# A retention layer with a two-matrix ELU block: one more first-GEMM product by quarter products, with ScalarE seeding the rounds

## The chip, the core and the metric

The kernel runs on one core of a Trainium2 chip. The metric is the time of one execution on the device in microseconds (us); of several runs the median counts. The engines are TensorE (PE: matmuls, which accumulate in PSUM), VectorE (DVE) and ScalarE (ACT) (elementwise work and copies out of PSUM and into it), GpSimd (POOL) and SyncE (SP, which here issues all DMAs). Each engine works through its own instructions; they wait for one another by semaphores.

## What is computed

```python
def _attn_ref(q, k, v):                       # B, H, S, D = 4, 8, 768, 64
    gamma = 1.0 - 2.0 ** (-5.0 - np.arange(H))
    state = zeros(B, H, D, D)
    for t in range(S):
        state = gamma * state + einsum('bhd,bhe->bhde', k[:, :, t], v[:, :, t])
        y[:, :, t] = einsum('bhd,bhde->bhe', q[:, :, t], state) / sqrt(D)

def _moe_ref(x, w_in, w_out):                 # x: 3072 tokens x 512, from y
    h = x @ w_in                              # w_in: 512 x 2048
    g = np.where(h > 0, h, np.exp(np.minimum(h, 0)) - 1)
    return g @ w_out                          # w_out: 2048 x 512
```

All of it is float32. A float32 matmul of the program shows in the profile as two MATMUL records, so counts in the profile are twice those of the code.

## The kernel before

The 3072 tokens are six blocks of 512. A retention step makes each block's x in chunks of 128 tokens: scores, states and outputs, small matmuls at L319, L359, L415 and L430, which the program scatters among the GEMMs. Block 0 and block 1 go first. Blocks 2 to 5 are joined to two large blocks of 1024 tokens, and the change lies in the loop over these two (`nb`, L1659 on), with small changes in block 1 so that retention steps fit.

Both GEMMs of a large block are split by Strassen and Winograd's scheme: seven products of half size, M1 to M7, in place of eight. C11 = M1 + M2, and the others add M6, M7, M5, M4, M3 to partial sums of these. The first GEMM of a large block does three of the seven, M2, M3 and M7, *by quarter products*: each is split by the same scheme once more. `big_twice` (L1146) does one half of such a product, in this order: quarter products 1, 2, 6 and 7, then 5, then 4, then 3, each of two matmuls of 128x256, with ScalarE copies out of PSUM (`lift`, L1170) and VectorE additions (`plus`, L1174) between them. It is a generator: the loop over `ORDER1` interleaves two of them, so that products 4 and 3 of one (its tail) come among the products of the next: 1, [4], 2, 6, 7, [3], 5. Product 6 accumulates in the PSUM bank that product 1 filled, so it must wait until ScalarE has copied product 1 out.

The other four, M1, M6, M4 and M5, are done plainly, in eight rounds (L1738 on). Round n handles one eighth of the features, tile n: `rest(n, j)` (L1206) is product j, two matmuls of 128x512. M1 starts the bank `qa`, M6 accumulates on it; ScalarE copies the bank (`seed`, L1672) to a second one, `qd`, on which M4 accumulates while M5 accumulates on `qa`. `sum_` (L1215, VectorE) adds the finished M2, M3 or M7 tile on the way out. The ELU of a tile is `begin` (L1221 and L1222: a Relu and an Exp by ScalarE into one of three tiles `r`) and `end` (L1223, VectorE). T3 = C22 - C12, an input of the second GEMM, is formed by `big_t3` (L1226) between the rounds.

`second_big` is the second GEMM of a large block: seven products in the order of `ORDER2`, each by seven quarter products (L1254) of four 128x256 matmuls. `next_big_input` (L1236) makes its inputs T2, T1 and T4 in place on VectorE, `input_parts` (L891 and L1127) their quarter sums. Retention steps of the next large block are put at its `VISITS`, loads of chunks at `LOADS`.

Nothing is scheduled by a planner: every engine gets its instructions in the order in which the program emits them (`manual_schedule`). The weights' sums are made on the chip (`combine_small` for the quarter products), sent to DRAM scratch (`send_small`) and fetched again into a ring of eight slots in the order of `want_first` and `want_second` (L829), the next fetch being issued when a product is done with its slot (`done`). For the first large block the plain parts are still in SBUF (`w_all`).

Of the kernel before, what the change touches and what calls it, by code (L numbers as in the profile page):

```python
# [19 lines left out]
def kernel(  # L20
# [764 lines left out]
    ORDER2 = [1, 2, 6, 7, 5, 3, 4]  # L785

# [19 lines left out]
    def want_second(tb):  # L806

        rest = []
        for j in ORDER2:
            mine = []  # L810
            for k in (1, 2, 6, 7, 5) + ((4, 3) if j == 4 and tb == NTB - 1 else (3, 4)):
                if k in SMALL:
                    n = SMALL[k]
                    mine.append(((tb, j, k), scratch2[SEVEN[j]][:, 512 * n : 512 * n + 512]))
                else:
                    mine.append(((tb, j, k), scratch[4 * SLOT[j] + {1: 0, 2: 1, 4: 3}[k]].rearrange("p c -> p c")))
            for x in mine[:2] + rest + mine[2:5]:
                want(*x)
            rest = mine[5:]
# [3 lines left out]
    blocked = {(2, "t", 7)}  # L823
# [14 lines left out]
    W_IN = {2: w_a_[:, :, :, 1], 3: w_x_[:, :, :, 1], 7: w_x_[:, :, :, 0]}  # L838
    AMONG = {2: 0, 3: 1, 7: 2}

    def combine_small(j):

        if j == 7:
# [30 lines left out]
    LAYER = {1: w_a_[:, :, :, 0], 4: w_b_[:, :, :, 1], 5: w_b_[:, :, :, 0], 6: w_y_}  # L874
    PLANE = {1: 0, 6: 1, 5: 2, 4: 3}
# [184 lines left out]
    def pair_of(x, n):  # L1060
        if x in G:
            return G[x][n // 2][:, n % 2]
        a, b = IN_W[x]
        return groups_of[:, n, a // 4 : b // 4 + 1 : b // 4 - a // 4, :, a % 2].rearrange("p g f t -> p f g t")

# [7 lines left out]
    ORDER1 = [(j, at) for j in (2, 3, 7) for at in range(2)]  # L1073
    AT = {1: (0, 0), 2: (0, 1), 6: (1, 0), 7: (1, 1), 5: (2, 0), 4: (2, 1), 3: (3, 0)}

    def want_first(n):
# [12 lines left out]
        for j, at in ORDER1:  # L1089
# [3 lines left out]
            if (j, at) == (3, 0):  # L1093
                layer(1, 0)
# [6 lines left out]
        layer(6, 0)  # L1101
        piece(*before, 3)
        for m in range(NQ):
            if m:
                layer(1, m)
                layer(6, m)
# [3 lines left out]
    big_xs, layer_x = {}, {1: xa[:, 0:2].rearrange("p k (h t) -> p k h t", h=2)}  # L1110

    def big_x(j):

        x, t = {2: xa, 3: xb2}[j], next_ts()
        yield from inner_x(j, t, *(x[:, 2 + k, TH * u : TH * u + TH] for k in range(2) for u in range(2)))
# [28 lines left out]
    PLACE = {2: "C11", 3: "C12", 7: "C22"}  # L1144
# [53 lines left out]
    def big_rest(n, m, j, ps):  # L1198
# [6 lines left out]
        for k in range(2):  # L1205
            nc.tensor.matmul(  # L1206
                ps, lhsT=w[:, k, :], rhs=layer_x[j][:, k], start=(j == 1 and k == 0), stop=(k == 1),
# [17 lines left out]
    def big_t3(n):  # L1225
        nc.vector.tensor_tensor(out=pair_of("T3", n), in0=pair_of("C22", n), in1=pair_of("C12", n), op=ALU.subtract)  # L1226

    def next_big_input(name):

        to, x, y, op = {  # L1230
            "T2": ("C11", "T3", "C11", ALU.add), "T1": ("C12", "C22", "C11", ALU.subtract),
# [7 lines left out]
    def second_big(nb, behind_last):  # L1239
# [54 lines left out]
        def inner_end(j):  # L1294
# [3 lines left out]
            k = kept2[7].rearrange("p (d t c) -> p d t c", d=2, t=2)  # L1298
# [32 lines left out]
        def sum_up(j, m):  # L1331
# [7 lines left out]
            elif j == 5:  # L1339
                add(m, kept2[6], m)  # L1340
                h = mpool.tile([P, 4 * TH], FP32, name="h", tag="m")
                add(h, m, kept2[7])
                store("C22", h)
                add(kept2[7], kept2[6], kept2[7])
            elif j == 3:
                add(m, kept2[5], m)
                store("C12", m)
            elif j == 4:
                add(m, kept2[7], m)
# [6 lines left out]
        for at, j in enumerate(ORDER2):  # L1356
# [8 lines left out]
            if j in (2, 6, 7):  # L1365
                some(changes, 2 if j == 2 else 1)
            if j == 1:
# [3 lines left out]
                next(cur)  # L1371
            parts = input_parts(ORDER2[at + 1]) if at + 1 < 7 else iter(())
            if j in (2, 5):

                some(parts, 2)
            else:
                for _ in parts:
                    pass
            if at == 6:
                behind_last()  # L1380
            if j != 1:
                next(cur)
                yield "middle"
                next(cur)
            for _ in parts:
                pass
            if j == 1:
                changes = itertools.chain(*(next_big_input(x) for x in ("T2", "T1", "T4")))
                some(changes, 2)
            elif j in (2, 6, 7, 5):  # L1390
                some(changes, 1 if j in (2, 6) else 2)
# [186 lines left out]
    smalls = {j: combine_small(j) for j in (2, 3, 7)}  # L1578
# [60 lines left out]
    LOADS = {(1, "first"): 0, (2, "end"): 1, (4, "end"): 2, (5, "end"): 3}  # L1639
    for s in sec:  # L1640
# [8 lines left out]
        if s == ORDER2[-1]:  # L1649
            break  # L1650
    for _ in sec:
        pass
# [6 lines left out]
    for nb in range(NB):  # L1659
# [4 lines left out]
        def rest(m, j):  # L1664
            if j == 1:
                qa[m] = ps_r.tile([P, 2, TH], FP32, name="qa", tag="r") if m in (0, 2 * NQ - 1) else bank("a")
            big_rest(nb, m, j, qd[m] if j == 4 else qa[m])
            if j == 6:
                qd[m] = bank("bd"[m % 2])

        def seed(m):
            nc.scalar.copy(qd[m], qa[m])  # L1672
# [4 lines left out]
        def begin(x, m):  # L1677
            ends[x, m] = big_elu(x, m)

        def end(x, m):  # L1680
            ends.pop((x, m))()

        def bring(tb, n):
# [3 lines left out]
        xparts = itertools.chain(big_x(3), big_layer_x())  # L1687
        stores = [
            lambda: [send_quarters(2)], lambda: [send_quarters(3)], lambda: [send_layer(4, range(NQ))],
            lambda: [send_layer(1, range(NQ))], lambda: [send_quarters(7), send_layer(6, range(NQ))],  # L1690
            lambda: [send_layer(5, range(NQ))],
        ]
        for at, (j, sub) in enumerate(ORDER1):
            if at == 2:
                rest(0, 1)
# [6 lines left out]
            some(xparts, {2: 1, 3: 4, 4: 1, 5: 1}.get(at, 0))  # L1702
            next(cur)
            if at == 5:
                sum_("C11", 0)
                begin("C11", 0)
            run(tail)
            if nb == 0 and at == 1:
                run(smalls[7])
                retention_step(3, 1)  # L1710
            next(cur)
            tail = cur
            if at == 0 and nb == 0:
                retention_step(3, 0)
            elif at == 1:
                if nb == 0:
                    retention_step(3, 2)
                    next(tail)
                    retention_step(3, 3)
                    for _ in tail:  # L1720
                        pass
                    retention_step(3, 4)
                some(xparts, 4)
            elif at in (4, 5) and more:
                bring(groups[0], at - 4)
            if nb == 0:
                stores[at]()
                send_small()
            if nb == 0 and at == 1:
                blocked.clear()  # L1730
                fetch()
        next(tail)
        run(xparts)
        end("C11", 0)

        sec = second_big(nb, (lambda: run(big_x(2))) if more else lambda: None)
        LAST = 2 * NQ - 1
        for n in range(2 * NQ):  # L1738

            if n < LAST:  # L1740
                rest(n, 6)
            if n == 0:
                for _ in tail:
                    pass
            if n:
                begin("C12", n - 1)
            if n < LAST:
                seed(n)
# [3 lines left out]
            if n < LAST:  # L1752
                if n:
                    end("C12", n - 1)
                if n in (3, 5):
                    big_t3((n - 3) // 2)
                rest(n + 1, 1)
                sum_("C11", n + 1)
                begin("C11", n + 1)
                if n:  # L1760
                    end("C22", n - 1)
            rest(n, 4)
            sum_("C21", n)
            if n == LAST:
                end("C12", n - 1)
            else:
                begin("C21", n)
                end("C11", n + 1)
            if n == LAST - 1:
                rest(LAST, 6)  # L1770
# [99 lines left out]
```

## Time and profile before

| | us |
|---|---|
| three runs | 627.43, 627.56 (median), 629.32 |
| the profiled execution: its time | 625.79 |
| its span, first to last instruction | 624.0 |

The span by stages of the program (busy us of each engine; windows of the trace):

| stage | from, to | length | PE | DVE | ACT |
|---|---|---|---|---|---|
| block 3's retention among the first quarter products | 240.0-261.9 | 21.90 | 20.67 | 14.30 | 4.35 |
| large block 1, rest of the quarter products | 261.9-284.5 | 22.60 | 22.60 | 13.40 | 8.95 |
| large block 1, rounds | 284.5-344.1 | 59.60 | 59.60 | 48.85 | 40.46 |
| large block 1, second GEMM | 344.1-440.6 | 96.50 | 95.65 | 77.83 | 13.24 |
| large block 2, quarter products | 440.6-483.0 | 42.40 | 42.40 | 21.63 | 15.28 |
| large block 2, rounds | 483.0-534.1 | 51.10 | 51.10 | 40.19 | 37.72 |
| large block 2, second GEMM | 534.1-620.3 | 86.20 | 86.20 | 67.85 | 15.00 |

How to read it: a stage in which PE is busy for its whole length is as short as its matmuls allow. PE's records overlap by some 0.17 us at each change of group, since matmuls are pipelined, so the distance between two starts, and not the length of a record, is what a matmul costs.

### The profile page before, as it was taken

The page shows a single profiled execution, that of the slowest core. Times are in us where ns is not written, and L with a number is a line of the kernel's source. Part 1 is how long each engine was busy: PE and PEld are TensorE (multiplying, and loading weights), DVE is VectorE, ACT ScalarE, POOL GpSimd, SP SyncE. Part 2 cuts the span into 40 slices and gives each one's busy share as a digit, 9 for nine tenths or more (in the row PEclk, how much of TensorE's full clock was granted, in tenths as well). Part 3 has the DMA queues.
Part 4 walks back from the last instruction along what each step waited for, and adds up shares of the span by engine and source line. Part 5 has one row for each costly group of instructions (what it writes and reads, how often), then busy time and mean ns, then how long its engine had stood idle before and what let it go on. Part 6 is the DMA issues. An engine that isn't in the chain of part 4 may idle for free.

```text
span 624.0 us, 13220 instructions
## 1 busy us (share of the span) xinstructions
PE 613.5 (98%) x5398; PEld 472.1 (76%) x5398; DVE 480.6 (77%) x754; ACT 248.2 (40%) x420; POOL 24.6 (4%) x30
## 2 busy tenths in 40 slices
PE   7999999999999999999999999999999999999997
PEld 5864568888888998786444888888888444788886
DVE  5779789989788876647788987976456688996783
ACT  5899635114531112135766301000233777511110
POOL 1012000000000010000200002100000000000000
PEclk9999999999999999999999999999999999999999
DMA  8698569699474997579500358644645222456562
GB/s 318 263 402 301 177 202 270 202 268 288 182 237 118 368 377 264 154 226 334 208 2 2 102 179 299 220 132 139 202 136 165 86 72 79 124 153 187 154 176 85
DMA packets 76172, 122.50 MB, mean 196 GB/s; under 512 B 5840, under 2 KB 44240, under 8 KB 71376
## 3 DMA queue, kind: packets, MB, share of 16 engines
q1 hardware_dynamic: 76112, 121.66, 59.8%
q8 instruction: 43, 0.70, 0.5%
q14 instruction: 17, 0.14, 0.1%
HBM read 92.80 MB, written 28.84 MB: 195 GB/s over the span
## 4 chain that ended last, share of the span: by engine, by line
PE 94%; DMA 2%; DVE 1%; issue 1%; SPq 0%; ACT 0%; DVEq 0%
PE pa L1254 15%; PE pa L1206 10%; PE pd L1254 7%; PE pa L1159 7%; PE pa L765 4%; PE pb L1254 4%; PE pa L921 4%; PE pa L542 3%; PE pd L1159 3%; PE qa L1206 3%; PE x L632 3%; DMA chunk<-in_qkv_dram 2%; PE pa L632 2%; PE pd L1206 2%; PE pb L1206 2%; PE pd L921 2%
## 5 line engine op out<-in xcount | busy, mean ns | idle before, releaser
L1262 ACT COPY ms<-pa 128x256 f32<-128x256 f32 x41 | 15.3, 373 | 111.4 <-PE pa L1254 111.4
L1254 PE MATMUL pa<-w_all,wq 128*128 128x256 f32 x184 | 43.3, 381 | 0.0
L1222 ACT ACTIVATE r<-r 128x512 f32<-128x512 f32 x64 | 40.3, 630 | 2.0
L1254 PEld LDWEIGHTS pa<-w_all,wq 128*128 128x128 f32 x184 | 34.7, 190 | 4.8
L293 POOL TENSOR_TENSOR chunk<-chunk,vf 128x512 f32<-128x512 f32 x16 | 21.6, 1347 | 361.5 <-DMA chunk<-in_qkv_dram 322.7
L1266 DVE TENSOR_TENSOR res<-pd,ms 128x256 f32<-128x256 f32 x26 | 11.0, 422 | 31.0 <-PE pd L1254 23.1
L1254 PE MATMUL pa<-gC,wq 128*128 128x256 f32 x136 | 32.5, 382 | 0.0
L1170 ACT COPY m<-pa 128x512 f32<-128x512 f32 x24 | 14.1, 586 | 44.1 <-PE pa L1159 44.1
L1254 PEld LDWEIGHTS pa<-gC,wq 128*128 128x128 f32 x136 | 25.5, 190 | 4.4 <-issue 1.0
L1254 PE MATMUL pa<-ts,wq 128*128 128x256 f32 x112 | 26.6, 380 | 0.0
L171 ACT ACTIVATE w_all<-wraw 128x1024 uint32<-128x1024 uint32 (+1 forms) x19 | 19.1, 1005 | 15.4 <-PE x L632 5.0
L1254 PE MATMUL pd<-ts,wq 128*128 128x256 f32 x104 | 24.7, 380 | 0.0
L1236 DVE TENSOR_TENSOR gC<-w_all,gC 128x1024 f32<-128x1024 f32 x20 | 24.2, 1243 | 0.0
L1254 PEld LDWEIGHTS pa<-ts,wq 128*128 128x128 f32 x112 | 21.2, 190 | 2.9
L173 ACT ACTIVATE w_all<-wraw 128x1024 fp8e4<-128x1024 f32 (+1 forms) x19 | 22.6, 1190 | 0.6
L1206 PE MATMUL pa<-gC,w_all 128*128 128x512 f32 x48 | 22.3, 596 | 0.0
L1221 ACT ACTIVATE r<-w_all 128x512 f32<-128x512 f32 x32 | 20.1, 627 | 4.7 <-DVE w_all L1215 4.5
L1254 PEld LDWEIGHTS pd<-ts,wq 128*128 128x128 f32 x104 | 19.7, 190 | 2.9 <-DVE res L1266 0.3
L1223 DVE SCALAR_TENSOR_TENSOR w_all<-r,w_all 128x512 f32<-128x512 f32 x32 | 21.9, 684 | 0.0
L1206 PE MATMUL pa<-ts,wq 128*128 128x512 f32 x48 | 21.7, 592 | 0.0
L542 PE MATMUL pa<-xb,w_all 128*128 128x512 f32 x48 | 21.5, 597 | 0.0
L201 DVE CUSTOM_DVE_ANT_0 w_all<-wraw,w_all 128x2048 uint16<-128x2048 uint16 (+1 forms) x19 | 20.1, 1057 | 0.8
(330 smaller groups left out, 1435.2 us busy)
## 6 DMA issues: line engine op xcount, KB each, us to landing
wq<-scratch_dram SPq DMA_DIRECT2D x187, 256.0 KB, 3.1
chunk<-in_qkv_dram SPq DMA_DIRECT2D x22, 1024.0 KB, 7.4
wraw<-in_w_dram SPq DMA_DIRECT2D x15, 1024.0 KB, 6.5
scratch_dram<-w_all SPq DMA_DIRECT2D x16, 256.0 KB, 3.8
scratch_dram<-gT SPq DMA_DIRECT2D x12, 256.0 KB, 4.3
out_dram<-res SPq DMA_DIRECT2D x5, 512.0 KB, 3.2
scratch_dram<-m SPq DMA_DIRECT2D x12, 192.0 KB, 5.8
wq<-scratch_dram SPq DMA_DIRECT2D x18, 128.0 KB, 2.9
```

Source lines behind the costliest of these rows:

```text
L173: nc.scalar.activation(top, hi.bitcast(FP32), AF.Copy, scale=2.0**-120, saturate=False)
L293: eng.tensor_tensor(out=v, in0=v, in1=vf[:, i].unsqueeze(2).to_broadcast([C, H, D]), op=ALU.mult)
L542: nc.tensor.matmul(hp, lhsT=w[n][:, fi, j // 2, j % 2, :], rhs=xb[:, j, :], start=(j == 0), stop=(j == 3))
L632: nc.tensor.matmul(X[j][:, d, :], lhsT=w[j][:, d * P : d * P + P], rhs=x[j], start=(n == 0 and d == 0), stop=at_end, skip_group_check=True,)
L765: nc.tensor.matmul(ps[:, fi, :], lhsT=w[:, fi, j2, :], rhs=x[:, j2, :], start=(begin and fi == 0 and j2 == 0), stop=(j2 == 1), skip_group_ ...
L921: nc.tensor.matmul(ps, lhsT=w[:, f, :], rhs=ts[j][k][:, f, :], start=(begin and f == 0), stop=(f == 3), skip_group_check=True,)
L1159: nc.tensor.matmul(ps[:, f, :], lhsT=w[:, f, :], rhs=big_xs[j][k], start=(begin and f == 0), stop=True, skip_group_check=True,)
L1206: nc.tensor.matmul(ps, lhsT=w[:, k, :], rhs=layer_x[j][:, k], start=(j == 1 and k == 0), stop=(k == 1), skip_group_check=True,)
L1222: nc.scalar.activation(r, r, AF.Exp, scale=-1.0)
L1223: return lambda: nc.vector.scalar_tensor_tensor(g, r, -1.0, g, ALU.add, ALU.max)
L1236: nc.vector.tensor_tensor(out=quarter(to, r, t), in0=quarter(x, r, t), in1=quarter(y, r, t), op=op)
L1254: nc.tensor.matmul(ps, lhsT=w[:, f, :], rhs=ts[j][k][:, f // 2, f % 2, :], start=(begin and f == 0), stop=(f == 3), skip_group_check=True,)
```

## The change

M1 of each large block, too, is now done by quarter products: `ORDER1` is M2, M3, M1, M7, two halves each, at 0 to 7 in the loop. Its result goes to two chunk buffers of the load pool (`held_x`, `G["M1"]`), from where `big_c11` (VectorE) adds it to M2 to make C11 in SBUF; the ELU of C11's eight tiles then runs before the rounds, begun by `begin("C11", ...)` at the ends of 5, 6 and 7 and once more behind the last half. The rounds keep M6, M4 and M5. As M1 no longer starts the bank `qa`, ScalarE copies the M1 tile from SBUF into it (`seed`), and M6 accumulates on that; the copy from `qa` to `qd` stays (`second_seed`). `qd` is one bank, `qa` takes three in turn. T3 is made in the second GEMM by `next_big_input`, whose products come in a new order (`BIG2`); its sums add in place, one addition fewer. The two M1 buffers are taken from the pool of four that the chunk loads use, so chunks 2 and 3 of the next retention block are loaded behind the rounds, and the retention steps move to later places in the second GEMM. Block 3's retention steps move by some products, too. M1's quarter sums are made, sent and fetched like those of M7, in the same buffer.

```diff
-    blocked = {(2, "t", 7)}
+    blocked = {(2, "t", 1), (2, "t", 7)}
...
-    AMONG = {2: 0, 3: 1, 7: 2}
+    AMONG = {2: 0, 3: 1, 7: 2, 1: 3}
...
-        if j == 7:
+        if j in (1, 7):
             t = gq["C22"].rearrange("p a t -> p (a t)").rearrange("p (k m c) -> p k m c", k=4, m=4)
...
-    ORDER1 = [(j, at) for j in (2, 3, 7) for at in range(2)]
+    ORDER1 = [(j, at) for j in (2, 3, 1, 7) for at in range(2)]
...
-                ps, lhsT=w[:, k, :], rhs=layer_x[j][:, k], start=(j == 1 and k == 0), stop=(k == 1),
+                ps, lhsT=w[:, k, :], rhs=layer_x[j][:, k], start=False, stop=(k == 1),
...
-    def big_t3(n):
-        nc.vector.tensor_tensor(out=pair_of("T3", n), in0=pair_of("C22", n), in1=pair_of("C12", n), op=ALU.subtract)
+    def big_c11(r, at):
+        g = G["C11"][r][:, at]
+        nc.vector.tensor_tensor(out=g, in0=g, in1=G["M1"][r][:, at], op=ALU.add)
...
-            "T2": ("C11", "T3", "C11", ALU.add), "T1": ("C12", "C22", "C11", ALU.subtract),
+            "T3": ("T3", "C22", "C12", ALU.subtract), "T2": ("C11", "T3", "C11", ALU.add), "T1": ("C12", "C22", "C11", ALU.subtract),
...
-            if j in (2, 6, 7):
-                some(changes, 2 if j == 2 else 1)
+            some(changes, {2: 1, 3: 4, 7: 1, 5: 2}.get(j, 0))
...
+            some(changes, {1: 1, 2: 2, 6: 3, 7: 2}.get(j, 0))
...
-    LOADS = {(1, "first"): 0, (2, "end"): 1, (4, "end"): 2, (5, "end"): 3}
+    LOADS = {(1, "first"): 0, (2, "end"): 1, (4, "middle"): 2, (5, "first"): 3}
...
         def seed(m):
+            qa[m] = bank("aab"[m % 3])
+            nc.scalar.copy(qa[m], tile_of("M1", m))
+
+        def second_seed(m):
+            qd[m] = bank("d")
             nc.scalar.copy(qd[m], qa[m])
...
+        def sent(j):
+            run(smalls[j])
+            send_small()
+            blocked.discard((2, "t", j))
+            fetch()
...
+            if at == 4:
+                held_x = [ldpool.tile([P, 2048], FP32, name="chunk", tag="chunk") for _ in range(2)]
+                G["M1"] = [x.rearrange("p (n f t c) -> p n f t c", n=2, f=2, t=2) for x in held_x]
             cur = big_twice(nb, j, sub)
             next(cur)
...
+            some(xparts, {2: 4, 3: 1, 4: 4, 5: 1, 6: 1, 7: 1}.get(at, 0))
+            if at == 1 and nb == 0:
+                retention_step(3, 2)
+            elif at == 6:
+                end("C11", 0, 1)
+            elif at == 7:
+                end("C11", 4, 5)
             next(cur)
+            if at == 1 and nb == 0:
+                retention_step(3, 3)
             run(tail)
+            if at in (5, 6):
+                big_c11(0, at - 5)
+                big_c11(1, at - 5)
             next(cur)
             tail = cur
+            if at >= 5:
+                begin("C11", *{5: (0, 1), 6: (4, 5), 7: (2, 3)}[at])
             if nb == 0:
+                if at == 0:
+                    retention_step(3, 1)
+                    sent(1)
+                elif at == 1:
+                    retention_step(3, 4)
+                    run(tail)
+                elif at == 2:
+                    sent(7)
...
+        seed(0)
+        end("C11", 2, 3)
+        next(tail)
+        rest(0, 6)
+        second_seed(0)
+        run(tail)
+        begin("C11", 6, 7)
+        seed(1)
         for n in range(2 * NQ):
 
             if n < LAST:
-                rest(n, 6)
+                rest(n + 1, 6)
...
             if n:
                 begin("C12", n - 1)
-            if n < LAST:
-                seed(n)
+            if n + 2 <= LAST:
+                seed(n + 2)
             if n:
                 begin("C22", n - 1)
                 end("C21", n - 1)
+                end("C12", n - 1)
+            else:
+                end("C11", 6, 7)
             rest(n, 4)
             sum_("C21", n)
+            if n < LAST:
+                second_seed(n + 1)
+            begin("C21", n)
+            if n:
+                end("C22", n - 1)
...
             rest(n, 5)
             sum_("C12", n)
             sum_("C22", n)
...
-        LOADS = [(1, "end"), (2, "first"), (2, "end"), (3, "first")]
+        LOADS = [(3, "middle"), (3, "end"), (4, "first"), (4, "middle")]
```

## The prediction

> **What bounds the kernel now.** I read the page's busy row and the shares of the chain that ended last first, then the timelines of PE, ACT and DVE in the first large block.
>
> ```profile
> PE 613.5 (98%) x5398; PEld 472.1 (76%) x5398; DVE 480.6 (77%) x754; ACT 248.2 (40%) x420; POOL 24.6 (4%) x30
> ...
> PE 94%; DMA 2%; DVE 1%; issue 1%; SPq 0%; ACT 0%; DVEq 0%
> ```
>
> The chain is PE nearly throughout: matmuls taken away are time won, and each new wait of PE is time lost at its full length. The timeline of PE gives prices (start, length, work, count, idle before it):
>
> ```profile
> 235.11 1.16 PE L921 MATMUL pa<-gC,wq 128*128 128x128 f32 x8 [0.35 <-ACT ms L929]
> ...
> 270.69 1.03 PE L1159 MATMUL pa<-xb,wq 128*128 128x256 f32 x4
> 271.56 1.03 PE L1159 MATMUL pa<-ts,wq 128*128 128x256 f32 x4
> 272.42 1.11 PE L1159 MATMUL pa<-ts,w_all 128*128 128x256 f32 x4
> 273.36 1.03 PE L1159 MATMUL pd<-ts,w_all 128*128 128x256 f32 x4
> ...
> 294.97 1.88 PE L1206 MATMUL pa<-xt,w_all 128*128 128x512 f32 x4
> 296.69 1.88 PE L1206 MATMUL pd<-ts,w_all 128*128 128x512 f32 x4
> ...
> 396.28 0.69 PE L319 MATMUL sc<-chunk 64*64 64x64 f32 x32 [0.84 <-DMA chunk<-in_qkv_dram]
> ```
>
> Start to start, a quarter product costs 0.863 us (270.69 to 271.56), 0.94 as the first of a half (272.42 to 273.36), and one `rest` 1.717 (294.97 to 296.69).
>
> ACT's timeline, in which everything runs in program order:
>
> ```profile
> 234.79 0.27 ACT L929 COPY ms<-pa 128x128 f32<-128x128 f32 x1 [1.52 <-PE pa L921]
> ```
>
> ```profile
> 271.75 0.59 ACT L1170 COPY gC<-pa 128x512 f32<-128x512 f32 x1 [0.28 <-PE pa L1159]
> ...
> 294.18 0.63 ACT L1221 ACTIVATE r<-gC 128x512 f32<-128x512 f32 x1 [0.37 <-DVE gC L1215]
> 294.84 0.63 ACT L1222 ACTIVATE r<-r 128x512 f32<-128x512 f32 x1
> 295.38 0.58 ACT L1672 COPY pd<-pa 128x512 f32<-128x512 f32 x1
> 295.90 0.62 ACT L1221 ACTIVATE r<-w_all 128x512 f32<-128x512 f32 x1
> ```
>
> Latencies follow. A copy starts 0.19 after the next product has started (271.56 to 271.75). Relu to Exp is 0.66, Exp to the next work 0.54, a copy to the next work 0.52: an ELU is 1.20 of ACT. PE goes on 0.05 after a copy's end (234.79 + 0.27 to 235.11). DVE's timeline prices the addition that makes C11, by an operation of equal shape on SBUF, and the steps from DVE to ACT (0.04: 296.89 + 0.69 to a Relu at 297.62) and from ACT to DVE (0.04: the Exp above, 294.84 + 0.63, to an ELU's last step at 295.51):
>
> ```profile
> 275.03 1.22 DVE L1127 TENSOR_TENSOR gC<-xb,xt 128x1024 f32<-128x1024 f32 x1
> ...
> 296.89 0.69 DVE L1215 TENSOR_TENSOR gC<-pa,gC 128x512 f32<-128x512 f32 x1 [0.69 <-PE pa L1206]
> ```
>
> **1. The matmuls of M1.** Removed per large block: eight `rest`, 8 x 1.717 = 13.74. Added: two halves of seven quarter products, 14 x 0.863 + 2 x 0.08 = 12.24. Gain 1.50, for two blocks **-3.0**. With them come, per block, eight copies out of PSUM and eight seeds (16 x 0.58 = 9.3 us of ACT), six additions of 0.69 and four `big_c11` of 1.22 (9.0 of DVE, against the eight `sum_` of C11 and T3's four subtractions that leave, 10.4). In a half, four copies in 6.1 us of PE are hidden as those of M2, M3 and M7 are now; what is not hidden is in 2.
>
> **2. ScalarE ahead of the rounds.** Call the eight halves 0 to 7, as the loop does; a product in brackets is one of the half before. The ELUs of C11 are not new work (ACT has the same 64 Relus and Exps), but they move to where PE waits for what is queued behind them. Each batch of two tiles is 2 x 1.20 = 2.40 of ACT, and is emitted after the copy of quarter product 3 (`lift` to its place), so it cannot start before that product ends; and everything that ACT does later for PE stands behind it. The chain from the end of product 3 to PE's release is copy 0.19 + 0.52, batch 2.40, then one more copy 0.58 + 0.05: 3.74. The seed, SBUF to PSUM, is not in the trace; nearest are the 0.57 to 0.59 of all copies with PSUM on one side or both and the 0.63 of activations on SBUF, so 0.58, with 0.05 either way. What PE has in between differs:
>
> - After the last half: [3], then `rest(1, 6)`, which accumulates on seed 1, emitted behind `begin("C11", 6, 7)`. No cover: 3.74.
> - Before: [3] of half 6, then 5 and [4] (1.73), then `rest(0, 6)`, which waits for seed 0 behind `begin("C11", 2, 3)`: 3.74 - 1.73 = 2.01.
> - In half 7: product 6 accumulates on product 1's bank and waits for its copy, which is behind `begin("C11", 4, 5)`. Cover 5, 1, [4], 2 = 3 x 0.863 + 0.94 = 3.53: 0.21.
> - In half 6: the same, but the Relu first waits for `big_c11`, which itself waits for the copy of product 3: 0.19 + 0.59 + 0.04 + 1.22 + 0.04 + 2.40 + 0.58 + 0.05 = 5.11, less 3.53: 1.58.
>
> PE executes matmuls in program order, so none of its later work can fill these. The sum is 7.54 per block, **+15.1**. From above: a `big_c11` that runs beside POOL's scaling of a chunk may take 1.85, as L1127 did at 286.33 (POOL from 286.06), so 0.6 more per block. From below: only the two waits for seeds are beyond doubt, since nothing but one or two products lies in between: 11.5. In the stage windows PE is now busy for 22.60 of 22.60 us and 59.60 of 59.60 us, so no old wait takes them in.
>
> **3. The rounds.** PE per round 3 x 1.717 = 5.15. ACT: three ELUs and two copies, 3.60 + 1.04 = 4.64 by starts, 3.78 + 1.16 = 4.94 by lengths. DVE six operations some 0.60 apart. `second_seed(n + 1)` waits for `sum_` of C21 (0.9 after `rest(n, 4)`), and PE needs it only two `rest` later (3.43 in all); the seeds are two rounds ahead. I take 0; were ACT the bound by lengths with a wait of 0.5 per round, 0.3 x 16 = 5.
>
> **4. Second GEMM.** T3 is four DVE operations of 1.24 (L1236), in place of those between the rounds; DVE has 77.8 of 96.5 us there, and in the densest step, M3 (four changes, four quarter sums, the small sums: some 11 of 12.1 us), the sums end about 1 us before their first user. 0; without that cover some 1 us per block. The wait of 0.84 for a chunk goes: the last load (389.10, landing after 7.13 us) had three quarter products of 1.73 before its scores, now five, 8.6: **-0.84**. Against it the four loads come in 12 us rather than 19: up to +1.
>
> **5. Block 3's retention.** DVE now does the states (4.9 us from 248.97, the start of their matmuls, to 253.85), then M1's four combines (2.5) and the sum that frees `pd` (0.7), 8.1 in all, against 7.2 of PE before it needs `pd`: +0.9. M7's combines stand likewise before such a sum: 0.2 + 0.6 + 2.5 + 0.7 = 4.0 against 3.53: +0.5. Old idle times of 0.87 and 0.36 in this stage (before 256.73 and 260.02) go or stay: net **+0.5**, from -1.2 to +1.7. (The 7.2 are states 2.03, a first product 0.94, [4] 0.86, half of the outputs 1.59 by 252.06 to 253.65, then two products.) A chunk asked for earlier pushes weights back in a stage (222 to 242) whose DMAs are 98.5% busy: 0 to +1.7, taken as 0, since it would land (7.3 after its issue) some 0.5 ahead of its scores. M1's extra 12 sends and 6 fetches, and 0.8 MB more fetched in the second large block, lie under 12 us more of quarter products at a rate that made no wait in the second block's quarter products (161 GB/s from 440.6 to 483.0): 0. The two chunks loaded into M1's buffers wait for seeds 3 and 7; the later of these is issued in round 5, two rounds (10 us) before the second GEMM, and its chunk is first used 8.6 us into that: 0.
>
> **Sum:** -3.0 + 15.1 - 0.84 + 0.5 = +11.8. The profiled execution took 625.79 (span 624.0 and 1.8 around it) and would become 637.6; on the median of 627.56, **639.3**.
>
> The trace starts with a cold TensorE: its first two 512-wide matmuls take 1142 ns each (L1405), later ones 592 to 605. The Trainium skill, page TensorE: Matmul & The Clock Gate (Part 1), says that one idle window of about 3.4 us halves TensorE's clock until it has been busy for such a window again. No later part of this trace shows it: idle there is at most 0.87, and the granted clock 0.999. By that rule a wait of 3.74, if it happens to hold a whole window, would cost an estimated 1.7 to 3.4 more, and the sum would be up to 646; without the rule it stays as it is.
>
> **Rivals.**
>
> *Matmuls decide (faster).* If ScalarE's queue were never late, the sum would be -3.0 - 0.84 + 0.5: 624.2. The place is the change from quarter products to rounds; it decides if the waits of part 2 stay below 3.3 in both blocks together. For it: ACT is 40% busy. Against: the wait at `rest(1, 6)` alone is 2 x 3.74.
>
> *Only the seeds wait.* If DVE or ACT are sooner in halves 6 and 7 than I reckon, 11.5 remains: 635.7.
>
> *ScalarE becomes the bound of the rounds.* Then +5 on top: 644. For it: 4.94 of 5.15. Against: the same instructions start 0.52 and 0.54 after one another in the trace.
>
> *The change doesn't do what it says*, as M1's ELUs could still run in the rounds: excluded by the order of emission.
>
> **How the numbers follow.** Forecast 0.70, only the seeds 0.10, ScalarE in the rounds 0.12, matmuls decide 0.05, near no change 0.03. About 0.3% (1.9 us) is what a measurement can tell: faster 0.05, same 0.03, slower 0.92. The range takes the lower bounds (627.56 - 3.0 + 11.5 - 0.84 - 1.2 = 634) and the ScalarE rival (644), with 1 us around: 633 to 645.
>
> **What would show it.** Right: in each large block four PE idle times with ACT as releaser, near 1.6 and 0.2 before L1150, 2.0 and 3.7 before L1197 (the changed lines of quarter products and `rest`); rounds of 5.15; no wait for a chunk near 400. Wrong: PE busy throughout the change to the rounds, or idle times spread over the rounds.

## The result, and the profile after

| | us |
|---|---|
| kernel before, median of 4 runs | 627.64 (627.43 to 629.32) |
| changed kernel, median of 4 runs | 652.04 (650.32 to 655.10) |
| ratio, with its 95% interval | 1.0388, 1.0338 to 1.0438 |
| profiled execution of the changed kernel (its span) | 650.32 (648.5) |

The change makes the kernel 24.4 us slower. The prediction said slower, with 639.3 us and a range of 633 to 645: the direction was right, the size half of what came. The profiled executions differ by 24.5 us (650.32 and 625.79), so the two traces show the whole of it.

First the page of the changed kernel: the busy row, the granted TensorE clock in forty slices of the span, and the shares of the chain that ended last.

```profile
PE 618.2 (95%) x5446; PEld 482.8 (74%) x5446; DVE 494.2 (76%) x770; ACT 263.0 (41%) x452; POOL 24.5 (4%) x30
...
PEclk9999999999999999999999799999999989999999
...
PE 85%; DVE 5%; ACT 4%; DMA 3%; issue 2%; DVEq 0%; SPq 0%
```

PE was busy for 98% of its span before and is now for 95%; the chain, 94% PE before, has DVE, ACT and DMA in it. New, too, are two slices in which TensorE was not granted its full clock. PE's waits, the longest first (operation, who released it, us in total, times, longest), say where:

```profile
PE pa L1197 <- ACT pa L1650: 10.7, 4, 3.5
PE sc L319 <- DMA chunk<-in_qkv_dram: 5.1, 2, 3.7
PE pa L1150 <- ACT m L1161: 2.8, 2, 1.4
PE sc L319 <- issue: 2.2, 1, 2.2
```

L1650 is the seed, L1197 `rest`, L1150 a quarter product of the first GEMM, L1161 the copy that lifts one, L319 the scores. The first and the third row are the predicted waits for ScalarE; the second is for chunks of input. For the fourth, inside the scores of block 3, the profile names no releaser ("issue"). PE's timeline (start, length, operation, count, idle before it) has them in place, in both large blocks:

```profile
303.41 1.98 PE L1197 MATMUL pa<-ts,w_all 128*128 128x512 f32 x4 [1.81 <-ACT pa L1650]
305.23 1.03 PE L1150 MATMUL pa<-ts,wq 128*128 128x256 f32 x4
309.79 1.98 PE L1197 MATMUL pa<-ts,w_all 128*128 128x512 f32 x4 [3.53 <-ACT pa L1650]
...
363.21 1.13 PE L319 MATMUL sc<-chunk 64*64 64x64 f32 x32 [3.65 <-DMA chunk<-in_qkv_dram]
365.75 1.13 PE L319 MATMUL sc<-chunk 64*64 64x64 f32 x32 [1.41 <-DMA chunk<-in_qkv_dram]
366.81 3.25 PE L1246 MATMUL pa<-w_all,wq 128*128 128x256 f32 x8
369.90 1.89 PE L1246 MATMUL pb<-w_all,wq 128*128 128x256 f32 x8
...
518.67 2.92 PE L1197 MATMUL pa<-gC,wq 128*128 128x512 f32 x4 [3.53 <-ACT pa L1650]
521.38 2.69 PE L1197 MATMUL pd<-w_all,wq 128*128 128x512 f32 x4
523.90 1.88 PE L1197 MATMUL pa<-ts,wq 128*128 128x512 f32 x4
```

Three things are to be seen. The waits before `rest` are 1.81 and 3.53. The scores at 363 and 365 wait for chunks, which they never did in the second GEMM before beyond 0.84. And after such waits the *same* work takes longer: eight matmuls of L1246 at 366.81 last 3.25 where the next eight last 1.89; two `rest` from 518.67 to 523.90 take 5.23 from start to start, 1.8 more than twice 1.717, where the first block's pair at 309.79 takes 3.54. In the window from 520 to 526 the granted clock was 0.75, in that from 352 to 370 it was 0.81.

ACT's timeline before the wait of 3.53 shows the queue order that makes it: after the copy of the last quarter product (L1161) come two ELUs (L1212 and L1213, of which the first and the last instruction are shown), and only then the seed (L1650) for which PE waits.

```profile
306.29 0.59 ACT L1161 COPY w_all<-pa 128x512 f32<-128x512 f32 x1 [0.29 <-PE pa L1150]
306.77 0.63 ACT L1212 ACTIVATE r<-gC 128x512 f32<-128x512 f32 x1
...
308.62 0.63 ACT L1213 ACTIVATE r<-r 128x512 f32<-128x512 f32 x1
309.16 0.58 ACT L1650 COPY pa<-chunk 128x512 f32<-128x512 f32 x1
```

SP's timeline shows the second cause (the length of a row covers several issues):

```profile
308.86 48.22 SPq L830 DMA_DIRECT2D wq<-scratch_dram  x5
357.17 0.86 SPq L113 DMA_DIRECT2D chunk<-in_qkv_dram  x2
```

SP issues five fetches of weights in 48 us, because the later ones wait for PE to leave a slot of the ring (one such wait, for a product of L1246, is 41.4 us long), and the two chunk loads behind them go out together at 357.17, 1.2 us before PE begins the scores.

With the starts of the stages' first products as borders, the two traces give this ledger. "Moved" is the work of retention steps that changed stage (2.02 of block 3's scores, 4.0 of block 4's scores and states, at PE's own durations).

| stage (start before, after) | before | after | difference | made up of |
|---|---|---|---|---|
| up to large block 1 (0, 0) | 237.00 | 242.57 | +5.57 | moved +2.02; waits of 0.85 for DVE and 2.21 inside the scores |
| block 1, first GEMM (237.00, 242.57) | 107.04 | 106.81 | -0.23 | moved -6.0; matmuls -1.0; ScalarE +7.4 |
| block 1, second GEMM (344.04, 349.38) | 96.48 | 107.44 | +10.96 | moved +4.0; chunks +5.1 -0.84; slow clock +2.2 |
| block 2, first GEMM (440.52, 456.82) | 94.96 | 103.13 | +8.17 | matmuls -1.0; ScalarE +7.4; slow clock +1.8 |
| block 2, second GEMM (535.48, 559.95) | 88.52 | 88.55 | 0 | |

### The profile page after: what moved, and what is told of

It is laid out like the page before. It is cut to its first block, busy times and chain, and to the rows that moved or that the text cites. A ratio compares the mean times of both kernels' runs of the same rounds, so it can differ in the third digit from the quotient of the medians.

```text
span 648.5 us, 13426 instructions
## 1 busy us (share of the span) xinstructions
PE 618.2 (95%) x5446; PEld 482.8 (74%) x5446; DVE 494.2 (76%) x770; ACT 263.0 (41%) x452; POOL 24.5 (4%) x30
## 4 chain that ended last, share of the span: by engine, by line
PE 85%; DVE 5%; ACT 4%; DMA 3%; issue 2%; DVEq 0%; SPq 0%
PE pa L1246 15%; PE pa L1150 8%; PE pd L1246 7%; PE pa L1197 6%; PE pd L1197 4%; PE pa L765 4%; PE pb L1246 4%; PE pd L1150 4%; PE pa L542 3%; PE x L632 3%; DMA wq<-scratch_dram 2%; PE pa L632 2%; PE pb L1197 2%; PE pa L922 2%; PE pd L765 2%
## 5 line engine op out<-in xcount | busy, mean ns | idle before, releaser
L1213 ACT ACTIVATE r<-r 128x512 f32<-128x512 f32 x64 | 40.3, 630 | 2.0
L1246 PE MATMUL pa<-gC,wq 128*128 128x256 f32 x168 | 40.3, 383 | 0.0
L1246 PE MATMUL pa<-w_all,wq 128*128 128x256 f32 x152 | 37.2, 391 | 0.0
L1161 ACT COPY m<-pa 128x512 f32<-128x512 f32 x32 | 18.7, 583 | 45.3 <-PE pa L1150 45.3
L1246 PEld LDWEIGHTS pa<-gC,wq 128*128 128x128 f32 x168 | 31.3, 190 | 6.0 <-DVE w_all L1206 1.3
L1246 PEld LDWEIGHTS pa<-w_all,wq 128*128 128x128 f32 x152 | 29.5, 196 | 4.4 <-ACT ms L1254 0.2
L1150 PE MATMUL pa<-ts,wq 128*128 128x256 f32 x104 | 26.9, 386 | 1.4 <-ACT m L1161 1.4
L1246 PE MATMUL pa<-ts,wq 128*128 128x256 f32 x112 | 26.9, 383 | 0.0
L1214 DVE SCALAR_TENSOR_TENSOR gC<-r,gC 128x512 f32<-128x512 f32 x24 | 16.2, 689 | 11.4 <-ACT r L1213 11.4
L1246 PE MATMUL pd<-ts,wq 128*128 128x256 f32 x104 | 24.6, 379 | 0.0
L1206 DVE TENSOR_TENSOR w_all<-pd,w_all 128x512 f32<-128x512 f32 x16 | 11.1, 691 | 17.1 <-PE pd L1197 17.1
L1150 PEld LDWEIGHTS pa<-ts,wq 128*128 128x128 f32 x104 | 19.1, 190 | 6.7 <-ACT m L1161 3.1
L1246 PEld LDWEIGHTS pa<-ts,wq 128*128 128x128 f32 x112 | 20.9, 190 | 3.3 <-ACT ms L1254 0.5
L319 PE MATMUL sc<-chunk 64*64 64x64 f32 x768 | 15.1, 232 | 7.3 <-DMA chunk<-in_qkv_dram 5.1
L1246 PEld LDWEIGHTS pd<-ts,wq 128*128 128x128 f32 x104 | 19.8, 190 | 2.7
```

The source lines that it names most:

```text
L1150: nc.tensor.matmul(ps[:, f, :], lhsT=w[:, f, :], rhs=big_xs[j][k], start=(begin and f == 0), stop=True, skip_group_check=True,)
L1213: nc.scalar.activation(r, r, AF.Exp, scale=-1.0)
L1214: return lambda: nc.vector.scalar_tensor_tensor(g, r, -1.0, g, ALU.add, ALU.max)
L1246: nc.tensor.matmul(ps, lhsT=w[:, f, :], rhs=ts[j][k][:, f // 2, f % 2, :], start=(begin and f == 0), stop=(f == 3), skip_group_check=True,)
```

## Experiments

All kernels are the changed kernel with the edit shown. Times are medians, each with the ratio to the kernel before that ran on the same chip beside it.

### The order of ScalarE's queue before the rounds

**e1_seeds.** The first two seeds go ahead of the ELUs.

```diff
-            qa[m] = bank("aab"[m % 3])
+            qa[m] = bank("aba"[m % 3])
...
             tail = cur
+            if at == 7:
+                seed(0)
+                seed(1)
...
-        seed(0)
         end("C11", 2, 3)
...
         begin("C11", 6, 7)
-        seed(1)
```

> The first two seeds are emitted in half 7, ahead of its batch of ELUs, in a bank that is free by then; all else stays. My theory: the two waits before `rest` (1.81 and 3.53 us per block, PE's L1197, ScalarE as releaser) are queue order alone. They go, 2 x (1.97 + 3.70) = 11.3 us by starts, and with the last of them the slow stretch of the second block behind the wait of 3.53 (1.8): -11 to -13 against the change, about 640. The wait near 1.4 at quarter products in half 6 stays, or grows by at most the 1.2 of two more copies. Rival (ScalarE's amount of work between halves 5 and round 0 is the bound, whatever its order): the waits reappear at the first rounds or in half 7, and less than 4 us are won.

652.50 us, ratio 1.0396 (1.0358 to 1.0433): nothing gained. The waits before `rest` did go, from 10.7 us in all to 0.4, but another of 8.4 in all came. PE's timeline at the start of the second GEMM, and DVE's:

```profile
353.19 2.93 PE L1246 MATMUL pb<-gC,wq 128*128 128x256 f32 x8 [4.21 <-DVE w_all L1206]
```

```profile
350.72 1.22 DVE L892 TENSOR_TENSOR w_all<-gC,ts 128x1024 f32<-128x1024 f32 x1
351.86 0.68 DVE L1206 TENSOR_TENSOR gT<-pb,gT 128x512 f32<-128x512 f32 x1
```

With the order a, b, a the last round uses bank b, and the second product of the second GEMM wants that bank. The sums that free it (L1206) stand in DVE's queue behind additions for the second GEMM (the line before it is the last of them). That was either the bank of this edit or lateness saved up in the rounds, which the next run tells apart.

**e1b_seeds.** The same with the banks in the order b, a, a.

```diff
-            qa[m] = bank("aba"[m % 3])
+            qa[m] = bank("baa"[m % 3])
```

> As e1_seeds, but the rounds take their banks in the order b, a, a, so that the last round's sums are made in bank a, as in the change itself; in e1_seeds they were in b, which the second product of the second GEMM uses, and PE waited 4.2 us per block there. My theory: the waits before `rest` are gone (10.7 to about 0.4) and so are the new ones at L1246 (8.4 to 0): -11.3 against the change and -1.8 to -4 of clock with them, about 637 to 640. Rival (DVE or ScalarE is the bound in the rounds, and the 4.2 in e1_seeds were lateness saved up in the rounds): a wait of 2 us or more stays at the change from rounds to the second GEMM, in whatever bank, and the time stays over 645.

639.96 us, ratio 1.0198 (1.0160 to 1.0237), 12.1 less than the change. Of the waits before `rest` 0.7 in all is left (0.33 at a second seed in each block), and no wait is left at the change to the second GEMM. ScalarE has the same work as in the change; the order of its queue was the cause, and the loss of e1_seeds was its bank.

**e2_begins.** The ELUs of halves 5 and 6 go behind the copy of product 1 of the next half.

```diff
             some(xparts, {2: 4, 3: 1, 4: 4, 5: 1, 6: 1, 7: 1}.get(at, 0))
+            if at in (6, 7):
+                begin("C11", *{6: (0, 1), 7: (4, 5)}[at])
...
-            if at >= 5:
-                begin("C11", *{5: (0, 1), 6: (4, 5), 7: (2, 3)}[at])
+            if at == 7:
+                begin("C11", 2, 3)
```

> The batches of ELUs of halves 5 and 6 are emitted one half later, behind the copy of product 1 that PE's quarter products wait for; seeds and the last two batches stay. My theory: the waits of 1.4 and 0.16 at L1150 in halves 6 and 7 go: 2 x 1.55 + 2 x 0.16 = -3.4, while the waits of 1.81 and 3.53 before `rest` stay. Rival (ScalarE's amount of work is the bound): what is won in halves 6 and 7 is lost again before `rest`, whose waits grow by as much, and the sum is 0.

The waits are as the theory has them: 2.8 in all at L1150 is gone, 10.7 before `rest` is unchanged. The time is 650.76 us (646.50 to 652.37), ratio 1.0352 (1.0300 to 1.0404): 1.3 less than the change where 3.4 were expected, and not to be told from it by these intervals. In the profiled execution both waits of 3.53 were followed by a slow stretch of some 6.4 us in place of 3.54; in that of the change only the second was, by one of 5.23. That takes back some 4 us. The waits are gone; the size of the gain isn't shown by this run alone.

### The order of SP's queue

**e3_loads.** The two chunk loads are asked for in the rounds.

```diff
             sum_("C12", n)
             sum_("C22", n)
+            if more and n in (2, 5):
+                bring(groups[0], 2 + (n == 5))
...
-        if more:
-            bring(groups[0], 2)
-            bring(groups[0], 3)
```

> The third and fourth chunk load of the next group are asked for in rounds 2 and 5, not at the head of the second GEMM. My theory: they were late because they stand in SP's queue behind four weight fetches that wait for PE to free their place in the ring; asked for before these, they land in time, the waits of 3.65 and 1.41 before the scores go (-5.1), and with the first of them the slow stretch of TensorE behind it (363 to 370 us, -2.2): -7.3 against the change where the clock falls there, -5.1 where it doesn't. Rival (the DMA engines are busy and the two loads are slow wherever they are asked for, or weights come later for it): the wait moves to the weights or stays over 2 us, and less than 3 us are won.

645.92 us, ratio 1.0287 (1.0259 to 1.0316), 6.1 less than the change, and no wait for a chunk in the second GEMM. SP's timeline:

```profile
319.96 20.93 SPq L113 DMA_DIRECT2D chunk<-in_qkv_dram  x2
```

The buffers come free at 320 and 341 (issues 20.93 us apart), so the loads could have landed well before their scores at 358. In the change they stood behind fetches that couldn't be issued yet. The transfers were not slow: from issue to landing it was 7.0 us in the change and is 4.8 here.

### The granted clock

**e6_half.** One ELU fewer ahead of the second seed.

```diff
-        begin("C11", 6, 7)
+        begin("C11", 6)
         seed(1)
+        begin("C11", 7)
```

> The last batch of ELUs is split: one tile ahead of the second seed, one behind it; all else as the change. The wait of 3.53 before the second round's `rest` becomes 2.33, 2 x 1.20 = -2.4. On top of it the clock: if it is the length of the wait that slows TensorE afterwards (over some 3.4 us), the slow stretch near 520 us goes (-1.8 where it occurred). Rival (any idle time can do it): a slow stretch stays behind the wait of 2.33 in one of the two blocks, and the clock is as low as in the change.

649.99 us, ratio 1.0353 (1.0326 to 1.0380), 2.1 less than the change; the clock is 0.987 to 0.992 in its four runs. PE's timeline:

```profile
303.30 1.03 PE L1150 MATMUL pa<-ts,wq 128*128 128x256 f32 x4
306.68 3.57 PE L1197 MATMUL pa<-ts,w_all 128*128 128x512 f32 x4 [2.35 <-ACT pa L1650]
...
518.12 3.66 PE L1197 MATMUL pa<-gC,wq 128*128 128x512 f32 x4 [2.35 <-ACT pa L1650]
```

The wait is shorter as reckoned, 2.35. But the four matmuls behind it take 3.57 and 3.66 instead of 1.98, one in each block. So a wait does not have to be over 3.4 us for TensorE to slow down, as the expectation had it.

**e7_warm.** e3_loads with work added inside the wait of 3.53: a product that nobody reads.

```diff
         for n in range(2 * NQ):
 
+            if n == 0:
+                idle, w = bank("b"), where[(nb + 2, "r", 6, 0)].rearrange("p (f k d) -> p f k d", f=2, k=2)[:, 0] if nb else LAYER[6][:, 0, 0]
+                for k in range(2):
+                    nc.tensor.matmul(
+                        idle, lhsT=w[:, k, :], rhs=layer_x[6][:, k], start=(k == 0), stop=(k == 1), skip_group_check=True,
+                    )
             if n < LAST:
                 rest(n + 1, 6)
```

> e3_loads with one product more per large block: two matmuls (four in the trace) into a free bank, whose result nobody reads, between PE's last quarter product and the `rest` that waits 3.53 us for the second seed. They need nothing but what PE has, so they run inside that wait: it becomes about 1.8 after 1.72 us of work, and the queue's order, ScalarE's and DVE's work are the same. My theory: what e3_loads shows beyond its waits is TensorE's clock, slowed by the idle time there (0.83 in the window 500 to 520 us and 0.92 in 305 to 350). With the wait half filled the clock stays near 0.999 and the time falls by 2 x 1.7 = 3.4 against e3_loads: 642 to 643, with more work on PE. Rival (the matmuls behind the waits are slow for another reason, or the clock falls for the two waits of 1.8 as well): the same 646 and a clock of 0.987 to 0.989.

639.61 us, ratio 1.0179 (1.0153 to 1.0204): PE has more to do, and the kernel is 6.3 us faster than e3_loads. PE's timeline there (L1742 is the added product), and then that of e3_loads:

```profile
305.62 1.88 PE L1742 MATMUL pb<-ts,w_all 128*128 128x512 f32 x4
309.32 1.98 PE L1197 MATMUL pa<-ts,w_all 128*128 128x512 f32 x4 [1.82 <-ACT pa L1650]
311.14 1.88 PE L1197 MATMUL pd<-ts,w_all 128*128 128x512 f32 x4
```

```profile
308.93 3.78 PE L1197 MATMUL pa<-ts,w_all 128*128 128x512 f32 x4 [3.53 <-ACT pa L1650]
312.50 3.18 PE L1197 MATMUL pd<-ts,w_all 128*128 128x512 f32 x4
```

PE goes on at the same time in both, 4.56 us after the start of its last quarter product, so the seed is as late as before; but the two `rest` behind it take 3.54 instead of 6.58 (to the next one's start at 315.51). Two times 3.0 is nearly all of the 6.3. The clock of the four runs is 0.999 to 1.0, in e3_loads 0.987 to 0.989. So the loss of clock is worth 3.0 us at each of these two places, and waits of 1.81 and 1.82 with 1.7 of work between them do not cause it.

### All three, and block 3

**e5_three.** The edits of e1b_seeds, e2_begins and e3_loads together.

> The edits of e1b_seeds, e2_begins and e3_loads together. My theory: the queue orders account for -11.3 -3.4 -5.1 and, as no wait over 1.5 us is left, the slow stretches of TensorE go too (clock 0.999 as before, not 0.987 to 0.992; some -4): 628, from 625 to 630, so about the kernel before. Rival (lateness is only moved on): over 635, with new waits in the rounds or at their ends.

627.24 us (10 runs), ratio 0.9997 (0.9971 to 1.0023): 24.8 less than the change, no difference to the kernel before, and the clock at 0.997 to 1.0. So three queue orders and what the clock does after their waits account for the whole net loss. In its profiled execution block 3's stage is still 3.8 longer than in that of the kernel before, and the whole is 2.4 longer (628.20 and 625.79); the medians don't show it. The sum of the single gains is 12.1 + 1.3 + 6.1 = 19.5; what is missing fits the slow stretches that each of those runs still had, but was not split further. What is left of waits before the rounds, from PE's timeline:

```profile
296.91 1.13 PE L1150 MATMUL pd<-gC,wq 128*128 128x256 f32 x4 [0.27 <-DVE w_all L1165]
...
305.38 1.98 PE L1197 MATMUL pd<-ts,w_all 128*128 128x512 f32 x4 [0.34 <-ACT pd L1654]
```

**e4_scores.** Only block 3's last scores move, behind the rest of block 1's second GEMM.

```diff
-    retention_step(3, 0)
     for _ in sec:
         pass
+    retention_step(3, 0)
```

> The last retention step of block 3 is emitted behind the remaining quarter products of M2's side work and not ahead of them, as little later as that allows (about 1.7 us of PE). My theory: the wait of 2.21 us for the last chunk inside the scores (236.14 to 242.2) shrinks by the work put ahead of it: -1.7 to -2.2. Rival: the chunk's transfer is later for the same reason (stage limited by its DMAs), and nothing is won.

653.03 us, ratio 1.0396 (1.0364 to 1.0427): no gain. The wait of 2.21 went, but there were waits of 0.78 for weights and of 1.38 without a named releaser earlier in the stage, where the profile of the change has none and one of 0.36. Such waits come and go: in the other runs above, with the same program order up to there, they are 0 to 0.91 and 0.3 to 1.44. The first quarter product starts at 241.92 (242.57 in the change).

**e8_block3.** e5_three with block 3's retention where the kernel before has it.

```diff
-    LOADS = {(1, "first"): 0, (2, "end"): 1, (4, "middle"): 2, (5, "first"): 3}
+    LOADS = {(1, "first"): 0, (2, "end"): 1, (4, "end"): 2, (5, "end"): 3}
...
-    retention_step(3, 0)
...
-            if at == 1 and nb == 0:
-                retention_step(3, 2)
...
-            if at == 1 and nb == 0:
-                retention_step(3, 3)
             run(tail)
+            if at == 1 and nb == 0:
+                retention_step(3, 1)
...
-                    retention_step(3, 1)
+                    retention_step(3, 0)
...
-                    retention_step(3, 4)
+                    retention_step(3, 2)
+                    next(tail)
+                    retention_step(3, 3)
                     run(tail)
+                    retention_step(3, 4)
```

> e5_three with block 3's retention back where the kernel before has it: its third and fourth chunk asked for at (4, end) and (5, end) as before, the scores behind the first half of quarter products, states and outputs one half later. In e5_three the first quarter product starts at 242.85, of which 2.02 are the scores; before it was 237.00, so this stage costs 3.8 us there (waits of 0.85 for DVE, 0.86 and 1.44 for issue, 0.79 for weights). My theory: those come from the two chunks asked for earlier (DMAs nearly saturated, POOL's scaling beside DVE's combination of products) and go: -2 to -3.8 against e5_three, 624 to 625.5, faster than before by the M1 term of 3.0. Rival (the lost 3.8 only moves into the quarter products, as the outputs then come later, or is M1's additional traffic): 626.5 to 628, no difference to e5_three.

629.29 us (12 runs), ratio 1.0017 (1.0002 to 1.0032): the rival. The stage up to the first quarter product is shorter by 3.0 (239.82 instead of 242.85, of which 2.02 are moved scores), and the quarter products take it back with waits of 1.13, 0.34, 0.96 and 0.17, most of them for DVE. With retention and loads ordered as in the kernel before, the stage is still 2.8 longer than there (237.00); 1.59 of that are two waits for weights near 221, which the trace of the kernel before doesn't have.

**e10_later.** e5_three with the edit of e4_scores, and the two chunks asked for one step later.

```diff
-    LOADS = {(1, "first"): 0, (2, "end"): 1, (4, "middle"): 2, (5, "first"): 3}
+    LOADS = {(1, "first"): 0, (2, "end"): 1, (4, "end"): 2, (5, "middle"): 3}
```

> e5_three with the scores of block 3's last retention step behind the remaining quarter products of the side work (as in e4_scores) and its third and fourth chunk asked for one step later each ((4, end), (5, middle)). My theory: the last small loss of e5_three against the kernel before is in block 3 (0.85 waiting for DVE beside POOL's scaling, 0.86 for the chunk inside the scores); both go, -0.9 to -1.7, so 625.5 to 626.5, 0.3% under the kernel before. Rival (e8_block3 has shown that waits in this stage only change places): 627 to 628.5, not to be told from the kernel before.

627.24 us (12 runs), ratio 1.0004 (0.9988 to 1.0020). The waits of 0.85 and 0.86 are gone from the profiled execution, whose span is 624.3 (a wait of 0.22 for the last chunk is new), but the median doesn't move. No version here is faster than the kernel before by more than the measurement can tell.

## Why the prediction was half right

**ScalarE ahead of the rounds: right in place and size.** Predicted were 1.58, 0.21, 2.01 and 3.74 per block, 7.54 in all. From start to start the trace has 1.55, 0.16, 1.97 and 3.70, 7.38 in all, the same in both blocks; e1b_seeds and e2_begins take them away one by one. That holds for the rival of the matmuls deciding, too: its condition was that these waits stay below 3.3 in both blocks, and they were 14.8.

**The rounds: right.** PE needs 5.15 per round by starts, without a wait, so ScalarE doesn't become the bound there.

**The second GEMM, T3: right**; the second one of block 2 takes 88.55 where it took 88.52. The old wait of 0.84 near 400 is gone as predicted.

**The failed step** is the sentence "The two chunks loaded into M1's buffers wait for seeds 3 and 7; the later of these is issued in round 5, two rounds (10 us) before the second GEMM, and its chunk is first used 8.6 us into that: 0." It reckons when the buffers come free, and takes that for the time of the loads. The buffers did come free then (e3_loads issues at 320 and 341), but the program asks for the chunks only behind the second GEMM's first products, whose fetches of weights wait on SP for PE. The issue was at 357.17, and PE waited 5.1 us; asked for in the rounds, the loads cost no wait (e3_loads, 6.1 less in the median). The cover was read from the buffer and not from the queue. This is the largest of the parts that make the 12.7 us by which the sum falls short (24.5 against 11.8).

**A term left out of the sum: the clock.** The prediction named a cost of 1.7 to 3.4 us by the Trainium skill, page TensorE: Matmul & The Clock Gate, Part 1, and left it out, since nothing in the trace of before showed it after the start. The runs do: some 4 us in the profiled execution (2.2 behind 363, 1.8 behind 518, none behind the wait at 309), 6.3 between e3_loads and e7_warm. That page has the watching window run freely, so that it is chance where a wait falls in it; the change's runs spread from 650.32 to 655.10 with clocks of 0.992 to 0.987, which agrees. So does a wait of 3.53 that was followed by slow matmuls five times out of eight in four profiled executions. The page wants one idle window of about 3.4 us, though, and here 2.35 were enough (e6_half, in both blocks): the measurement decides. The predicted range had room for this term or for the chunks, but not for both.

**Block 3: mis-sized.** Predicted were +0.5, and "0 to +1.7, taken as 0" for the chunk asked for earlier. The new waits of 0.64 and 0.53 stand against old ones of 0.87 and 0.36, so that part is about 0; but the stage before it is longer by 3.5 (5.57 less the moved 2.02). The prediction had no term for the two waits that make up most of this. One is the wait of 2.21 inside the scores. The scores of one chunk are 32 records; here are those of the change, and POOL's work on the last chunk, which starts when that has landed:

```profile
236.14 1.62 PE L319 MATMUL sc<-chunk 64*64 64x64 f32 x94
239.97 0.79 PE L319 MATMUL sc<-chunk 64*64 64x64 f32 x34 [2.21 <-issue]
```

```profile
236.77 1.04 POOL L293 TENSOR_TENSOR chunk<-chunk,vf 128x512 f32<-128x512 f32 x1 [5.21 <-DMA chunk<-in_qkv_dram]
```

The last chunk was there by 236.77; PE stops at 237.76, two records before the end of the third chunk, and goes on 3.2 us after the last one's landing. So the wait is not for a chunk, as the expectation of e4_scores takes it to be, and the prediction's 0 for the earlier load holds in this execution. What PE waited for is not shown. In the other runs that wait was 0.6 to 3.0 long with the same program order up to there, so part of it is chance. The other wait is that of 0.85 for DVE: an addition (L892, at 230.58) took 1.53 instead of 0.69 while POOL scaled the third chunk (230.40 to 231.57). In e2_begins and e7_warm POOL begins only after that addition has begun, the addition takes 0.68, and the wait is not there. The three attempts to win the stage back (e4_scores, e8_block3, e10_later) gained nothing in the median; what sets its length is left open.

**M1's matmuls: a little mis-sized.** In block 2's first GEMM, by starts and without the waits and the slow clock named above, the quarter products take 49.20 (56.58 less 7.38) where they took 36.57, so the fourteen new ones cost 12.63 and not 12.24; the `rest` take 41.31 where they took 54.94, 13.63 less and not 13.74. The gain is 1.0 per block, not 1.5. And in e5_three, where everything else is mended, this stage takes 94.79 (443.05 to 537.84) where it took 94.96: the wait of 0.34 for the second seed costs 0.50 by starts, and small ones the rest. Even with good orders the exchange of eight `rest` for fourteen quarter products brings next to nothing here.

Put together, the predicted +11.8 with 5.1 for the chunks, about 4.0 for the clock, 3.0 more for block 3, 1.0 less gain from the matmuls and 0.3 less from ScalarE makes 24.6; 24.5 were seen.

## What to carry to other kernels

A transfer starts when its queue reaches it and not when its buffer is free: whenever loads move, read what stands ahead of them in the issuing queue, and what that waits for. On an engine that works in order, put what another engine waits for ahead of work that only has to be done some time; moving two copies per large block ahead of ELUs that nobody waited for yet was worth 12 us here without any change in the amount of work. And where the matmul engine has hardly ever been idle, count for a new wait of more than 2 us not only its length but also a possible loss, here up to 3 us, to slower matmuls behind it.

## What the hardware showed beyond that

TensorE's granted clock fell behind waits of 2.35 (twice in e6_half), 3.53 and 3.65 us, but not behind each of them. The wait of 3.53 before `rest` was followed by slow matmuls in both blocks of e2_begins and e3_loads and in the second of the change, but not in the first of the change nor in either block of e4_scores. The clock didn't fall behind 1.82 (e7_warm), nor behind 1.38 or 1.39 alone. Nor is the length of the wait what decides between 2.2 and 3 us, as the wait inside block 3's scores shows, first in e7_warm, then in e1_seeds:

```profile
239.50 0.79 PE L319 MATMUL sc<-chunk 64*64 64x64 f32 x34 [2.55 <-issue]
```

```profile
241.66 1.33 PE L319 MATMUL sc<-chunk 64*64 64x64 f32 x34 [3.00 <-issue]
```

Behind 2.55 the 34 records take the same 0.79 as behind 2.21 in the change, at a granted clock of 1.00 (239 to 245 in both traces); behind 3.00 they take 1.33, at 0.66 (241 to 246). The 2.35 of e6_half that did slow TensorE came 2.8 us of work after another wait of 1.81; the 2.21 and 2.55 had no more than 0.85 of idle time in the 8 us before them. Whether that made the difference was not tried. The slow stretch is up to 6.6 us long (e3_loads, 308.93 to 315.51). And a matmul whose result nobody reads, put into such a wait, made the kernel 6.3 us faster.
